# A linear-attention and feed-forward kernel on one core: the hand-written start in another order

## The chip, the cores and the metric

The kernel runs on one core of a Trainium2 chip. The metric is device time in microseconds, from three runs of the same program. A core has a matrix engine (TensorE, PE in the rows, with PEld for its weight loads), a vector engine (VectorE, DVE), an activation engine (ScalarE, ACT), a general engine (GpSimd, POOL), and a queue that issues transfers (SyncE, SP). Each engine runs its own instructions strictly in the order in which they were written; the engines meet only through semaphores.

## The reference, cut to what matters

```
# attention: 4 x 8 heads, 768 steps, head dimension 48, float32
for t in range(S):
    cur = einsum('bhd,bhe->bhde', u * k[t], v[t])
    y[t] = einsum('bhd,bhde->bhe', r[t], state + cur)
    state = w[t] * state + einsum('bhd,bhe->bhde', k[t], v[t])
# feed-forward on the 3072 rows of y, 384 wide
h = x @ w_in            # 384 x 2048
out = (h * cos(h)) @ w_out
```

## The kernel before

The 768 steps are cut into chunks of 128; 4 batches give 24 chunks, and two chunks make a block (256 rows of x, 12 blocks). Inside a chunk the recurrence becomes matrix products: a backward and a forward scan of the decays on VectorE (L283, L289), a multiplication of k and r by the decays (L298), scores on TensorE (L374), a mask (L335 on GpSimd, L393 on VectorE) and the product with v (L479, L485). The state that a chunk passes on is a product of transposed keys and v (L444). The block's result lands in two PSUM banks called py; ScalarE copies them to the tile xT as the upper half of x (L171), and the rest is made as the lower half (L528 with L531, or L174 on VectorE).

The feed-forward goes over 16 slices of the weights (weight 0 to 15; two of them make a unit of the first product). A slice is fetched packed (L180) and unpacked by ScalarE (L191, L195, L171) and VectorE (L203, L205), or for weight 1 by TensorE and ScalarE (L211, L212, L216). The first product is L594 (tile ph), the gate h*cos(h) runs over ScalarE (L557), VectorE (L560), ScalarE (L573), VectorE (L574), the second product is L612.

The first 135 us or so are ordered by hand: the string START is a list of tokens that are carried out one after the other, and each writes its instructions to the ends of their engines' queues. The words used below, with the number of a chunk, block or weight behind them:

- `ld` loads a chunk, `e` and `f` are the backward and forward scan, `q` the product r*k (L272), `k` and `r` the products with the decays, all on VectorE; `pc` the bonus sums on TensorE (L311), `cd` their copy on ScalarE, `c` the bonus sum on VectorE for later chunks (L325); `a` the scores, `A` the mask on GpSimd, `P` its use on VectorE;
- `t` transposes the keys on TensorE (L408), `K` copies them on ScalarE (tile kn), `s` makes the state's sums on TensorE (L444), `n` copies them on ScalarE (L452); `o` is the product with v; `xh`, `xp`, `xa`, `xl` make the two halves of x;
- `wl`, `wg`, `wy`, `wc`, `wx` are the steps of a weight in this order (ScalarE, ScalarE, VectorE, ScalarE, VectorE), `wp` and `wv` stand for `wx` where TensorE makes it; `raw` and `v` issue transfers on SP;
- `m0.3` and `m1.3` are the two halves of the first product of unit 3, `I S N M H L` the gate's steps, `mm2.3` the second product; `D6` is six products into a bank that nobody reads.

Unit 0 and 1 belong to block 0 (weights 0, 1 and 2, 3), unit 2 and 3 to block 1 with the same weights. So the first product can start when x of block 0 (chunks 0 and 1) is there, and its unit 2 when x of block 1 (chunks 2 and 3) is there. Four buffers hold v: that of chunk 3 is loaded into the one that `s0` reads first.

Of the kernel before, what the change touches and what calls it, by code (L numbers as in the profile page):

```python
# [993 lines left out]
```

## Time and profile before

| | |
|---|---|
| median of 3 runs | 497.75 us (497.69 to 498.51) |
| the profiled execution, its own time | 497.51 us |
| its span in the trace | 495.7 us |
| TensorE, VectorE, ScalarE, GpSimd busy | 98%, 79%, 52%, 44% of the span |
| granted TensorE clock | 1.00 in every slice of the page |

The span is the part that the trace covers; 1.8 us of the execution's own time lie outside it. Busy TensorE is not TensorE at its peak, since matmuls are pipelined and their ends are modelled: what counts is the time from one group's start to the next, and the waits. Names in the rows are without buffer numbers; a row with x14 merges fourteen instructions, and its second column is the time from the first one's start to the last one's end. Engines overlap neighbouring instructions by some 0.1 us, so the step from one start to the next is a little shorter than an instruction's time.

### The profile page before, as it was taken

What the parts mean: (1) busy time and instruction counts of PE and PEld (TensorE: products, weight loads), DVE (VectorE), ACT (ScalarE), POOL (GpSimd) and SP (SyncE); (2) the same over time, 40 slices, a digit from 0 to 9 for tenths busy, and PEclk for the clock granted to TensorE, in tenths of its full rate; (3) what the DMA queues carried; (4) which work ended last, traced back from release to release, by engine and by line L of the source; (5) the groups of instructions that cost most, each with busy time, mean ns of one, the idle gap of its engine ahead of it and who ended that gap; (6) DMA issues with size and microseconds to landing.
All of it is one profiled execution on the core that took longest, in us unless ns stands there. A gap on an engine that the chain in (4) does not pass through costs nothing.

```text
span 495.7 us, 13535 instructions
## 1 busy us (share of the span) xinstructions
PE 486.5 (98%) x5560; PEld 471.9 (95%) x5560; DVE 393.6 (79%) x681; ACT 257.9 (52%) x444; POOL 216.5 (44%) x280
## 2 busy tenths in 40 slices
PE   8999999999999999999999999999999999999996
PEld 7789999999999899999999999999999999999996
DVE  7999899988979779869868968967966957587632
ACT  3899988445344444354445345345435535534542
POOL 5138798344336335244435344433624523432330
PEclk9999999999999999999999999999999999999999
DMA  8998830234454153153162150342222212023001
GB/s 284 414 395 298 343 104 9 60 104 127 124 165 122 20 196 80 18 199 78 17 197 54 45 198 19 78 125 91 73 94 107 65 32 98 33 67 126 34 1 36
DMA packets 46289, 58.59 MB, mean 118 GB/s; under 512 B 30736, under 2 KB 37392, under 8 KB 46224
## 3 DMA queue, kind: packets, MB, share of 16 engines
q1 hardware_dynamic: 46080, 57.59, 35.5%
q8 instruction: 45, 0.74, 0.6%
q14 instruction: 20, 0.16, 0.1%
q10 hardware_dynamic: 144, 0.10, 0.1%
HBM read 49.80 MB, written 4.72 MB: 110 GB/s over the span
## 4 chain that ended last, share of the span: by engine, by line
PE 75%; DVE 13%; ACT 4%; SPq 2%; DMA 2%; issue 2%; POOL 0%; DVEq 0%; ACTq 0%
PE ph L594 34%; PE acc L612 32%; PE pa L382 2%; PE py L479 2%; DVE rr L560 2%; DVE rr L574 2%; SPq L425 2%; PE py L485 2%; DVE tt L289 1%; PE py L513 1%; DVE h L203 1%; PE pst L444 1%; DVE ee L283 1%; ACT rr L557 1%; DMA tt<-tr 1%
## 5 line engine op out<-in xcount | busy, mean ns | idle before, releaser
L174 POOL TENSOR_TENSOR gs<-rr,gs 128x256 fp32r<-128x256 f32 x188 | 160.8, 877 | 221.9 <-ACT gs L171 215.3
L594 PE MATMUL ph<-xT,w 128*128 128x256 f32 x1728 | 219.5, 281 | 1.2 <-DVE rr L574 0.6
L594 PEld LDWEIGHTS ph<-xT,w 128*128 128x128 f32 x1728 | 212.3, 188 | 5.3 <-PE py L513 1.9
L612 PE MATMUL acc<-w,gs 128*128 128x384 f32 x1152 | 214.9, 337 | 0.0
L612 PEld LDWEIGHTS acc<-w,gs 128*128 128x128 f32 x1152 | 196.3, 188 | 0.1
L573 ACT ACTIVATE rr<-rr,quarter 128x512 f32<-128x512 f32 x96 | 69.5, 724 | 91.3 <-DVE rr L560 91.2
L560 DVE SCALAR_TENSOR_TENSOR rr<-rr,ph 128x512 f32<-128x512 int32 x96 | 65.5, 683 | 49.8 <-ACT rr L557 49.2
L171 ACT CAST gs<-rr 128x512 fp32r<-128x512 f32 x92 | 57.1, 620 | 72.7 <-DVE rr L574 49.2
L574 DVE TENSOR_TENSOR rr<-rr,ph 128x512 f32<-128x512 f32 x96 | 65.0, 678 | 21.3 <-ACT rr L573 19.3
L557 ACT ACTIVATE rr<-ph 128x512 int32<-128x512 f32 x96 | 57.2, 596 | 41.6 <-PE ph L594 41.1
L335 POOL TENSOR_SCALAR_AFFINE_SELECT asb<-cd 128x512 f32<-128x512 f32 x48 | 34.6, 745 | 42.5 <-DVE cd L325 24.3
L396 DVE COPY_PREDICATED asb<-turned_mask,pa 64x128 f32<-64x128 uint8 (+1 forms) x108 | 33.6, 346 | 2.1 <-POOL asb L335 0.3
L283 DVE TENSOR_TENSOR_SCAN ee<-tt,one_e 112x516 f32<-112x516 f32 (+1 forms) x25 | 32.9, 1315 | 1.7 <-DMA tt<-tr 1.7
L289 DVE TENSOR_TENSOR_SCAN tt<-tt,inj 112x516 f32<-112x516 f32 x24 | 30.3, 1263 | 0.8
L174 DVE TENSOR_TENSOR xT<-py,xT 128x384 fp32r<-128x384 f32 x22 | 11.3, 551 | 14.0 <-ACT xT L171 14.0
L195 ACT ACTIVATE top<-raw 128x768 f16<-128x768 bf16 x16 | 17.3, 1088 | 3.6 <-DMA raw<-wts 2.9
L479 PE MATMUL py<-asb,v 128*32 128x128 f32 x384 | 18.0, 276 | 0.3 <-DVE asb L393 0.2
L485 PE MATMUL py<-asb,v 128*32 128x128 f32 x384 | 17.3, 273 | 0.0
L203 DVE CUSTOM_DVE_ANT_0 h<-h,top 128x1536 uint16<-128x1536 uint16 x16 | 16.4, 1022 | 0.6 <-ACT h L191 0.6
L171 ACT CAST xT<-py 128x384 fp32r<-128x384 f32 x24 | 10.5, 481 | 9.3 <-PE py L513 5.1
L171 ACT COPY past<-dd 48x192 f32<-48x192 f32 x40 | 14.0, 349 | 2.7 <-DVE dd L358 2.4
L382 PEld LDWEIGHTS pa<-tt 48*64 48x64 f32 x576 | 12.9, 134 | 2.2 <-issue 2.0
(94 smaller groups left out, 358.5 us busy)
## 6 DMA issues: line engine op xcount, KB each, us to landing
tt<-tr SPq DMA_DIRECT2D x22, 770.5 KB, 7.1
raw<-wts SPq DMA_DIRECT2D x16, 767.8 KB, 7.3
rk<-tn SPq DMA_DIRECT2D x20, 384.0 KB, 4.5
v<-tv SPq DMA_DIRECT2D x24, 224.0 KB, 4.4
ww<-w SPq DMA_DIRECT2D x6, 768.0 KB, 4.5
out<-ob SPq DMA_DIRECT2D x23, 192.0 KB, 2.1
top<-tt SPq DMA_DIRECT2D x112, 16.0 KB, 1.8
top<-tt SPq DMA_DIRECT2D x112, 8.0 KB, 1.8
```

Of the source, the lines that this page charges most:

```text
L171: (nc.scalar.copy if E[name] is nc.scalar else E[name].tensor_copy)(out=out, in_=in_)
L174: E[name].tensor_tensor(out=out, in0=full, in1=high.bitcast(F32), op=ALU.subtract)
L283: nc.vector.tensor_tensor_scan(out=ee[:, pairs].rearrange("p a t -> p (a t)")[:, ::-1], data0=wp[:, cols][:, ::-1], data1=one_e[:, pairs]. ...
L289: nc.vector.tensor_tensor_scan(out=wp[:, 0:W129], data0=wp[:, 0:W129], data1=inj.rearrange("p a t -> p (a t)"), initial=0.0, op0=ALU.mult, ...
L335: nc.gpsimd.affine_select(out=asb, in_=col.unsqueeze(2).to_broadcast([C, NP, C]), pattern=[[0, 4], [1, C]], compare_op=ALU.is_equal, fill= ...
L396: nc.vector.copy_predicated(*(which(x) for x in (a["asb", h], turned_mask, pa[h])))
L557: nc.scalar.activation(made["rr"].bitcast(I32), ph, AF.Copy, scale=INV2PI / W_SCALE, bias=0.25)
L560: nc.vector.scalar_tensor_tensor(out=made["rr"], in0=made["rr"].bitcast(I32), scalar=-2.0 * math.pi * W_SCALE, in1=ph, op0=ALU.mult, op1=A ...
L573: N=lambda: nc.scalar.activation(made["rr"], made["rr"], AF.Sin, scale=1.0 / W_SCALE, bias=quarter),
L574: M=lambda: nc.vector.tensor_tensor(out=made["rr"], in0=made["rr"], in1=ph, op=ALU.mult), H=high, L=low)
L594: nc.tensor.matmul(out=ph[:, fi], lhsT=wgt[u * FU + fi][:, 0, a, kt * 128:(kt + 1) * 128], rhs=xT[:, b, kt], start=n == 0, stop=n == 3 * K ...
L612: nc.tensor.matmul(out=accs[i][j][:, :DM], lhsT=gs[:, a, fi, j * C:(j + 1) * C], rhs=wgt[u * FU + fi][:, 1, b], start=u == 0 and fi == 0 a ...
```

## The change

Only START changes. Two lines of it show the first part:

```
-ld0 e0 f0 ld1 raw2 raw1 q0 e1 k0 D14 pc0 r0 q1 cd0 v0 v1 raw0 f1 D10 a0 W0 wg2 wl2 A0 k1 pc1 wl1 r1 wy2 P0 cd1 D6 a1
+ld0 e0 f0 ld1 raw2 raw1 q0 k0 r0 e1 D14 pc0 cd0 v0 v1 raw0 f1 q1 D10 a0 W0 wg2 A0 k1 pc1 cd1 wl2 r1 P0 wl1 wy2 D6 a1
```

On VectorE chunk 0's `k0 r0` come ahead of chunk 1's `e1`, `q1` goes behind `f1`, `P0` ahead of `wy2`, and `wy0` ahead of `e3 q3`. On TensorE `t0 t1 s0` go from ahead of unit 0 to behind it, `wp1` ahead of `xp0.0`, and twelve new idle products, `D12`, stand in the place of `t0 t1`. ScalarE takes `cd1` ahead of `wl2`, both `xh` of block 0 ahead of `wc0`, and `K0 K1` and `n0` go to either side of `I0`. GpSimd's order stays. SP's stays until the transfers of v for chunks 6 and 7, which go behind others (they are not needed before 150 us).

TensorE, from the second filler ahead of `a1` to block 0's lower half, before (pt is `t0 t1`, py `o0` and then `xp0.0`, pst `s0`):

```order
L740 MATMUL filled<-ident 128x128 x6
L374 MATMUL pa<-tt 128x128 x8
L408 MATMUL pt<-ident,tt 128x112 x8
L479 MATMUL py<-asb,v 32x128 x8
L485 MATMUL py<-asb,v 32x128 x8
L479 MATMUL py<-asb,v 32x128 x4
L485 MATMUL py<-asb,v 32x128 x4
L479 MATMUL py<-asb,v 32x128 x4
L485 MATMUL py<-asb,v 32x128 x4
L528 MATMUL py<-xT,nident 128x384
L444 MATMUL pst<-v,kn 32x48 x2
```

The same engine and place after (left is `wp1`, ph with w_302 and w_262 are the halves of unit 0):

```order
L740 MATMUL filled<-ident 128x128 x12
L479 MATMUL py<-asb,v 32x128 x8
L485 MATMUL py<-asb,v 32x128 x8
L479 MATMUL py<-asb,v 32x128 x4
L485 MATMUL py<-asb,v 32x128 x4
L479 MATMUL py<-asb,v 32x128 x4
L485 MATMUL py<-asb,v 32x128 x4
L211 MATMUL left<-h,ident 128x384
L212 MATMUL left<-w_262,nident 128x384
L211 MATMUL left<-h,ident 128x384
L212 MATMUL left<-w_262,nident 128x384
L528 MATMUL py<-xT,nident 128x384 x2
```

The transposes and the state's sums have left this stretch, and follow unit 0; a row of L740 counts a product once that the trace counts as two instructions.

ScalarE, around the first `I0` (L557), before (L531 is `xa0.1`, L452 `n0`, L195 and L191 `wg3 wl3`, cd `cd2 cd3`, kn `K3 K2`):

```order
L531 CAST xT<-py 128x384
L452 COPY all_states<-pst 48x192 x4
L557 ACTIVATE rr<-ph 128x512
L195 ACTIVATE top_100<-raw 128x768
L191 ACTIVATE h<-raw 128x768
L171 COPY cd<-pc 128x8 x2
```

and after (the first kn is `K0 K1`, which stood far ahead before):

```order
L531 CAST xT<-py 128x384 x2
L216 CAST w_262<-left 128x384 x2
L171 COPY kn<-pt 128x384 x2
L557 ACTIVATE rr<-ph 128x512
L452 COPY all_states<-pst 48x192 x4
L195 ACTIVATE top_100<-raw 128x768
L191 ACTIVATE h<-raw 128x768
L171 COPY cd<-pc 128x8 x2
```

`K0 K1` and `n0` now stand between block 0's lower half and `wg3`, and `n0` behind `I0`.

The second part lies at unit 10. On VectorE (L560 is `S10`, L574 `M10`, L203 `wy13`, L325 `c4`, L393 `P5`):

```order
-L560 SCALAR_TENSOR_TENSOR rr<-rr,ph 128x512
-L203 ISA h<-h,top_100 128x1536
-L574 TENSOR_TENSOR rr<-rr,ph 128x512
+L205 TENSOR_TENSOR w_1076<-h,w_1076 128x2x384
+L560 SCALAR_TENSOR_TENSOR rr<-rr,ph 128x512
+L325 TENSOR_REDUCE cd<-rk 128x8
+L574 TENSOR_TENSOR rr<-rr,ph 128x512
+L203 ISA h<-h,top_100 128x1536
 L393 COPY_PREDICATED asb<-mask,pa 128x512 x2
 L560 SCALAR_TENSOR_TENSOR rr<-rr,ph 128x512
```

The bonus sum of chunk 4 takes the place between the two gate steps that weight 13's first step had; before, it came six instructions later, behind `r4`. On ScalarE `wg15` changes places with `wc13`. The transfers that turn chunk 4's keys (`t4`, L425) write the buffer that `c4` reads, and wait for it.

## Rows read from the trace of the kernel before

**Rows 1.** Table by stage: start:end, length, busy us of PE, PEld, DVE, ACT, POOL; clock, DMA share, GB/s.
```profile
10.00:36.00 26.00, 24.13 (x418) 20.65 (x417) 25.43 (x37) 22.31 (x43) 5.79 (x7) 1.00 1.01 404
```
**Rows 2.** TensorE's waits, a row: waiting line, what ended it, us in total, times, longest.
```profile
PE ph L594 <- DVE rr L574: 0.6, 1, 0.6
```
**Rows 3.** VectorE in order of time, 7 to 12 us: start, us, instruction.
```profile
7.28 1.23 DVE L283 TENSOR_TENSOR_SCAN ee<-tt,one_e 112x516 f32<-112x516 f32 x1 [0.64 <-DMA tt<-tr]
8.43 1.05 DVE L298 TENSOR_TENSOR tt<-tt,ee 112x512 f32<-112x512 f32 x1
9.41 1.11 DVE L298 TENSOR_TENSOR tt<-tt 112x512 f32<-112x512 f32 x1
10.45 0.68 DVE L272 TENSOR_TENSOR rkt<-tt 112x512 f32<-112x512 f32 x1
```
**Rows 4.** GpSimd in order of time: the masks of chunk 0.
```profile
8.02 1.96 POOL L335 TENSOR_SCALAR_AFFINE_SELECT asb<-cd 128x512 f32<-128x512 f32 x2 [2.02 <-ACT cd L171]
```
**Rows 5.** TensorE in order of time, 11 to 27 us.
```profile
11.67 1.05 PE L311 MATMUL pc<-u_by_head,rkt 112*128 112x2 f32 x8
12.58 1.58 PE L740 MATMUL filled<-ident 128*128 128x128 f32 x12
...
15.24 1.22 PE L408 MATMUL pt<-ident,tt 112*128 112x112 f32 x8
16.39 0.64 PE L479 MATMUL py<-asb,v 128*32 128x128 f32 x16
...
19.08 0.87 PE L444 MATMUL pst<-v,kn 128*32 128x48 f32 x64
19.88 0.91 PE L211 MATMUL left<-h,ident 128*128 128x384 f32 x2
...
21.63 0.95 PE L311 MATMUL pc<-u_by_head,rkt 112*128 112x2 f32 x8
...
23.79 1.93 PE L594 MATMUL ph<-xT,w 128*128 128x256 f32 x14 [0.23 <-ACT xT L531]
...
26.37 0.58 PE L408 MATMUL pt<-ident,tt 112*128 112x112 f32 x4
```
**Rows 6.** ScalarE in order of time, 17 to 36 us.
```profile
17.18 0.83 ACT L171 COPY kn<-pt 128x384 f32<-128x384 f32 x2
18.18 0.48 ACT L171 CAST xT<-py 128x384 fp32r<-128x384 f32 x1 [0.17 <-PE py L479]
...
23.61 1.29 ACT L452 COPY all_states<-pst 48x192 f32<-48x192 f32 x4
25.75 0.60 ACT L557 ACTIVATE rr<-ph 128x512 int32<-128x512 f32 x1 [0.85 <-PE ph L594]
26.25 1.09 ACT L195 ACTIVATE top<-raw 128x768 f16<-128x768 bf16 x1
...
34.28 0.86 ACT L171 CAST xT<-py 128x384 fp32r<-128x384 f32 x2
```
**Rows 7.** TensorE in order of time at the start of unit 2.
```profile
36.03 1.21 PE L594 MATMUL ph<-xT,w 128*128 128x256 f32 x8 [0.44 <-ACT wholes L171]
```
**Rows 8.** SP in order of time: v of chunks 2 and 3; the time includes a wait.
```profile
13.21 6.80 SPq L266 DMA_DIRECT2D v<-tv  x2
```
**Rows 9.** The page: DMA issues, KB each, median us from issue to landing.
```profile
raw<-wts SPq DMA_DIRECT2D x16, 767.8 KB, 7.3
```
**Rows 10.** VectorE in order of time, around unit 10's gate: `wy13`, then `M10`.
```profile
75.62 1.47 DVE L203 CUSTOM_DVE_ANT_0 h<-h,top 128x1536 uint16<-128x1536 uint16 x1
77.01 0.68 DVE L574 TENSOR_TENSOR rr<-rr,ph 128x512 f32<-128x512 f32 x1
```
**Rows 11.** In order of time: a gate step, `N10` on ScalarE; `c4`'s old place on VectorE.
```profile
63.47 0.60 ACT L557 ACTIVATE rr<-ph 128x512 int32<-128x512 f32 x1 [0.63 <-PE ph L594]
...
75.74 0.73 ACT L573 ACTIVATE rr<-rr,quarter 128x512 f32<-128x512 f32 x1 [0.75 <-DVE rr L560]
...
83.91 0.54 DVE L325 TENSOR_REDUCE cd<-rk 128x8 f32<-128x384 f32 x1
```

More of the change, by code (lines that the diff above doesn't have):

```diff
@@ L66 @@
 START = """
-ld0 e0 f0 ld1 raw2 raw1 q0 e1 k0 D14 pc0 r0 q1 cd0 v0 v1 raw0 f1 D10 a0 W0 wg2 wl2 A0 k1 pc1 wl1 r1 wy2 P0 cd1 D6 a1
-wc2 t0 wg1 A1 ld3 ld2 wg0 W1 t1 P1 v5 wx2 wy1 o0 K0 K1 xh0.0 xp0.0 s0 wl0 e3 q3 wc1 xa0.0 wy0 wc0 xh0.1 wp1 f3 pc3
-xp0.1 wv1 wx0 xa0.1 q2 e2 n0 k3 f2 raw3 k2 m0.0 m1.0 pc2 t3 r3 I0 r2 wg3 raw4 v2 wl3 cd2 v3 raw5 wy3 m0.1 cd3 S0 t2 a3
-A3 K3 K2 A2 P3 ld7 wl4 wg4 a2 ld5 wc3 wg5 N0 raw8 raw6 P2 s1 wx3 raw9 n1 o1 xh1.0 xl1.0 raw7 lr5 v4 ld4 m1.1 xh1.1
+ld0 e0 f0 ld1 raw2 raw1 q0 k0 r0 e1 D14 pc0 cd0 v0 v1 raw0 f1 q1 D10 a0 W0 wg2 A0 k1 pc1 cd1 wl2 r1 P0 wl1 wy2 D6 a1
+A1 wg1 wc2 D12 ld3 ld2 wg0 W1 P1 v5 wx2 wl0 wy1 wc1 o0 xh0.0 xh0.1 wy0 wc0 e3 wp1 xp0.0 xp0.1 wx0 xa0.0 xa0.1 wv1 q3
+f3 m0.0 m1.0 t0 t1 K0 K1 pc3 s0 q2 e2 k3 f2 raw3 k2 pc2 t3 r3 I0 n0 r2 wg3 raw4 v2 wl3 cd2 v3 raw5 wy3 m0.1 cd3 S0 t2
+a3 A3 K3 K2 A2 P3 ld7 wl4 wg4 a2 ld5 wc3 wg5 N0 raw8 raw6 P2 s1 wx3 raw9 n1 o1 xh1.0 xl1.0 raw7 lr5 v4 ld4 m1.1 xh1.1
 xl1.1 M0 m0.2 wl5 Wa3 I1 wy4 m1.2 S1 m0.3 H0 wc4 N1 wy5 wc5 wg6 I2 m1.3 M1 wx4 wl6 I3 Hv1 L0 mm2.0 m0.4 wx5 S2 N2 wy6
@@ L75 @@
 M8 I9 wc11 wy10 wg12 wc10 mm2.6 mm2.7 raw15 t5 d4 S9 N9 H8 m4 u4 r5 wx11 a5 wx10 M9 wl12 wl13 H9 L8 L9 m0.10 wy12 wc12
-m1.10 wg13 m0.11 I10 k4 wx12 S10 wy13 m1.11 N10 mm2.8 I11 M10 P5 wc13 wg15 wl15 Wa5 W4 d5 S11 wx13 N11 M11 f4 m0.12 r4
-c4 H10 L10 wg14 mm2.9 m1.12 m0.13 H11 t4 wl14 I12 S12 N12 pp4 pp5 wy15 m1.13 a4 L11 A4 M12 P4 I13 wy14 wcv15 S13 wx15
+m1.10 wg13 m0.11 I10 k4 wx12 S10 c4 m1.11 N10 mm2.8 I11 M10 wy13 P5 wg15 wc13 wl15 Wa5 W4 d5 S11 wx13 N11 M11 f4 m0.12
+r4 H10 L10 wg14 mm2.9 m1.12 m0.13 H11 t4 wl14 I12 S12 N12 pp4 pp5 wy15 m1.13 a4 L11 A4 M12 P4 I13 wy14 wcv15 S13 wx15
 mm2.10 wc14 mm2.11 o2 p2 N13 wx14 K5 m0.14 H12 m1.14 M13 m0.15 L12 xh2.0 Hv13 e6 k6 t6 m1.15 I14 S14 K4 N14 M14 mm2.12
```

## The prediction

> **What bounds the kernel now.** I read the table by stage first. Between 10 and 36 us VectorE is busy for 25.43 of 26 us, TensorE for 24.13, ScalarE for 22.31, and the DMA queues are full at 404 GB/s [rows 1]: in the start several engines are at their limit together, so a step gained on one can be lost on the next. The list of TensorE's waits then shows how little is left to take later: 0.6 us for a gate step of VectorE, once [rows 2], and 0.4 us at unit 2 put down to ScalarE's small copy called wholes [rows 7]. Behind block 0's first product TensorE runs one instruction behind the other, and over the whole span it is busy for 98%. So the end moves by what TensorE's long row of work is pushed or pulled, and the question is at which moment the row becomes unbroken, and which waits stand in it behind that. The views by time, engine by engine, show the moments: the row starts for good at 23.79 us, when the last quarter of block 0's x has come from ScalarE, and unit 0 ends 1.93 later, at 25.72 [rows 5].
>
> **VectorE's and TensorE's start.** Before, the scan `e1` waits 0.64 us for its transfer, ending at 7.28, and chunk 0's products `k0 r0` follow while GpSimd makes chunk 0's masks (8.02 to 9.98): they take 1.05 and 1.11 us. `q1`, a product of the same size that begins after the masks, takes 0.68 [rows 3, 4]. After, `k0 r0` go into that wait and lie before the masks: from 6.64 two steps of 0.6 (0.68 less the overlap of neighbours) end at 7.84. Then `e1` (step 1.15, from 7.28 to 8.43), 0.2 for the small reciprocal that a forward scan has ahead of it, `f1` as long as `e1`, and `q1`: 7.84 + 1.15 + 0.2 + 1.15 = 10.34, end 11.02. Before, `q1` ended at 11.13 without `f1`. So VectorE has gained a scan, 1.2 us, but the product that TensorE waits for next has gained only 0.1. `pc1` began at 11.67, since the scores `a0` stood ahead of it and waited for `r0` (end 10.52); `r0` is early now, and `pc1` can begin at 11.1, 0.55 earlier.
>
> From there TensorE's steps of before hold: from `pc1` to the place of `t0` 3.57 us (11.67 to 15.24), which gives 14.65. There `D12` stands now: the twelve instructions of `D6` took 1.58 [rows 5], so twenty-four take at most twice that, 3.16, and less by the end of the pipeline, which counts once and not twice, an estimated 0.3: I take 2.8. `o0` begins at 17.45 instead of 16.39. It is 1.06 later although its inputs are early; of the idle products every instruction counts, and nothing hides them. From `o0`'s start to `xh0.0` it was 1.79 (16.39 to 18.18) [rows 5, 6], so `xh0.0` begins at 19.25, while TensorE does `wp1` (19.88 to 21.63, 1.75) [rows 5]: 19.25 to 21.0. The two products of the lower half follow, some 0.4 each, and ScalarE's copies `xa0.0 xa0.1`, about 0.5 each as `xh0.0` [rows 6], partly beside them: ready at 22.1. Plus 1.93: unit 0 ends at 24.05, 1.65 us earlier than at 25.72. That gain is real, but it is made by putting work behind unit 0.
>
> **What comes behind unit 0.** On TensorE `t0 t1` (four transposes take 0.58, some 0.4 of it ahead of the next instruction), `pc3` (0.9, as `pc1`) and `s0` (0.80, from 19.08 to 19.88) [rows 5]: 2.4 us or a little more, so `s0` ends at 26.45, where before unit 0 had just ended, at 25.72: TensorE is later by 0.7 or 0.8. On ScalarE `K0 K1` (0.83), then `I0`, then `n0` (1.29), which must wait for `s0` [rows 6]. Before, `n0` filled the wait of ScalarE for unit 0 (23.61 to 24.90, with 0.85 of idle behind it): it cost nothing. Now it begins at 26.45 and `wg3`, the weight step behind it, at about 27.65 instead of 26.25: +1.4. Behind `wg3` ScalarE has had no rest up to `xh1.0` at 34.28, the copy of block 1's x, for which unit 2 waits; the little idle time in between gives back 0.2 at most, and `xh1.0` comes at 35.4 to 35.6. The masks of chunks 2 and 3 wait for `cd2 cd3`, copies in the same row of ScalarE, but end before `xh1.0`.
>
> The transfer of v for chunk 3 goes into the buffer that `s0` reads. Before, SP waited in the pair of v transfers, from 13.21 to 20.01 [rows 8]; now the wait lasts until `s0` has begun to read, about 25.9. Everything behind it in SP's row is issued up to 5.9 us later; the weight for `wg5`, which needs it at about 32.7, is the first at risk. By the median row, 7.3 us from issue to landing [rows 9], it would land at 33.6 and hold ScalarE 0.9; but that is the row of a full queue. This queue has run empty by then, and 767.8 KB at 404 GB/s are 1.9 us [rows 1, 9], so I take 30 to 31 and cost it at nothing; the end of the range is 0.9.
>
> **Unit 2.** Before, its row goes on at 36.03, ended by "ACT wholes" [rows 7], but that small copy feeds no product; x was ready at 35.14 (`xh1`, 34.28 + 0.86 [rows 6]). What holds the engine for these 0.9 us I can't read. Two bounds: if it is something that runs beside, and doesn't come later with x, the products wait only for x, 1.2 later than before, and TensorE loses 0.6 to 0.7 (its fifth product, on the lower half of x, goes from 36.4 to 37.05). If it follows x, the loss is the whole 1.2. The first is nearer to the 0.7 or 0.8 that TensorE already has from the moved work, so that both limits meet there.
>
> **Chunk 4's bonus sum.** `M10` on VectorE needs `N10`, which ends at 75.74 + 0.73 = 76.47 [rows 11]; before, it waited for `wy13` (75.62, 1.47 us), and ran from 77.01 [rows 10]. With `c4` (0.54 [rows 11]) in that place VectorE is free before `N10` ends, and `M10` begins at 76.52: 0.49 earlier. TensorE waits for it, 0.6 us [rows 2], so all of 0.49 is TensorE's. Could the start's loss vanish in this same wait, because TensorE comes to it later and VectorE doesn't? No: ahead of it the gate's first step on ScalarE waits 0.63 for TensorE's product (63.47 [rows 11]), so the gate goes with TensorE, and both are late alike. The bounds are 0, if VectorE comes 0.5 later than TensorE, and 0.5. `wy13` moves back by 1.1 and catches up when `c4`'s old place is reached at 83.91. `wg15` and `wc13` change places on ScalarE; `wc13` waits for `wy13`, so this is at zero.
>
> **The sum.** +0.7 (start) − 0.5 (gate) = +0.2 with the gap at unit 2 hidden, +1.2 − 0.5 = +0.7 with it not. The profiled execution took 497.51 us, 0.24 less than the median, 497.75. Against 497.51 the two are 497.7 and 498.2; the middle is 498.0, which I forecast. It is 0.25 above the median. A measurement of this kernel can tell about 0.2%, 1.0 us, from no change; this is inside. Its own range is 497.3 to 498.7.
>
> **Rivals.**
>
> *Faster: unit 0's gain survives.* If ScalarE were not late behind `n0`, because `K0 K1` and `s0` come sooner than I have it (x ready 1.65 earlier), x of block 1 would not be later, and VectorE's gained scan could bring it sooner by up to half of its 1.2 us (the other half goes where VectorE waits for TensorE's scores): the start would give −0.5, and with the gate −1.0 against 497.51: 496.5 to 496.7. For it: 1.65 us at unit 0, the largest single figure here. Against it: `n0` needs `s0`, and its 1.29 have lost their cover.
>
> *Slower: the scan under the masks.* The trace shows VectorE slowed beside the masks: 1.05 and 1.11 against 0.68 [rows 3, 4]. After, `e1` and `f1` run there. A scan with half a microsecond of overlap kept its 1.23 (`e1`, 7.28 to 8.51), hence my sum. But if `f1` is held until the masks end at 9.98 instead of starting at 9.19, then `q1`, `pc1`, unit 0, `s0`, `n0` and `xh1` are 0.8 later, all in one row: 498.0 + 0.8 = 498.8, up to 499.2 with the gap at unit 2 whole. It decides when the scans lose 0.75 together. The Trainium skill has a rule for this, in "SBUF — State Buffer", section "Who interferes with whom": a VectorE instruction with two inputs in SBUF contends with a GpSimd instruction that reads SBUF, and the shared port is an exclusive lock. By an exclusive lock `k0` would have been held at 8.43 until the first or second mask was over; it took 0.4 longer, not 1.5, so the row is nearer to a shared slowdown. By the rule the sum would be 498.8, by the row 498.0.
>
> *Slower: the queue.* SP held by v of chunk 3 until 25.9, and the weight for `wg5` late by 0.9: 498.9. It decides from a landing after 32.7 on. For it: the median row; against it: the empty queue.
>
> *Neither part does anything.* The moved steps find the same waits in another order: the median again, 497.75, inside my own range too.
>
> **Chances.** My sum and no effect at all, together 0.56; unit 0's gain survives 0.20; the scan under the masks 0.14; the queue 0.10. So faster 0.20, same 0.56, slower 0.24, and the range takes in nearly all of both sides: 496.6 to 499.2.
>
> **What would show it.** In the changed kernel's rows: `k0 r0` at 0.68 and ahead of `e1`, `f1` at 1.23 and `q1` ending by 11.1; twenty-four idle instructions from 14.65 to 17.45; unit 0's end at 24.05; `n0` at 26.45 and `wg3` at 27.65, with no wait between it and `xh1.0` at 35.4 to 35.6; v of chunk 3 issued at 25.9; in TensorE's waits, the one for L574 down from 0.6 to 0.2 or less. The forecast is wrong if `wg3` begins before 27, if `q1` ends after 11.8, or if unit 2 goes on before 36.2 or after 37.3.

## The result, and the profile after

The changed kernel takes 502.70 us (median of 6 runs, 502.19 to 504.54), against 497.76 before (497.49 to 498.51). The ratio is 1.0101, with a 95% interval from 1.0088 to 1.0114: 4.9 us slower, outside the range of 496.6 to 499.2. The profiled execution of the changed kernel took 503.11 us, with a span of 501.4 (before 497.51, with 495.7), so the traces lie 5.6 us apart, 0.7 more than the medians.

How late TensorE is, step by step, is read by comparing the start of the same product of the feed-forward (L594) in both traces:

| at product of L594 | before | after | later by |
|---|---|---|---|
| first of unit 0 | 22.93 | 22.20 | −0.73 |
| first of unit 1 | 26.72 | 28.62 | 1.89 |
| first of unit 2 | 35.32 | 39.03 | 3.71 |
| first of unit 3 | 38.13 | 41.33 | 3.20 |
| first of unit 8 | 61.17 | 65.14 | 3.97 |
| first of unit 12, behind unit 10's gate | 77.84 | 81.36 | 3.52 |
| first of units 13 and 14 | 82.11, 92.70 | 86.75, 97.81 | 4.63, 5.11 |
| from there to 360 us | | | 4.65 to 5.16 |
| last unit | 480.77 | 486.48 | 5.71 |

So nearly everything happens in the first 93 us: 1.9 before unit 1, 1.3 from there to unit 3, 0.8 more between units 6 and 7, where VectorE is full, and 1.1 net around unit 10, where the change was meant to gain. The last 0.6 come in one step, at 368 us of the trace before.

TensorE's rows by time, in the order start, duration, instruction, with the idle time ahead of it in brackets (they answer to [rows 5, 7]):

```profile
22.20 2.84 PE L594 MATMUL ph<-xT,w 128*128 128x256 f32 x18
...
30.96 2.06 PE L374 MATMUL pa<-tt 48*128 48x128 f32 x32 [0.67 <-ACT cd L171]
...
34.96 0.38 PE L479 MATMUL py<-asb,v 128*32 128x128 f32 x2
37.30 0.31 PE L479 MATMUL py<-asb,v 128*32 128x128 f32 x3 [1.96 <-issue]
...
37.87 5.72 PE L594 MATMUL ph<-xT,w 128*128 128x256 f32 x45
```

Unit 0 ends at 25.04 (22.20 + 2.84), earlier than before as forecast, though by 0.7 and not by 1.65. The third and fourth rows are the surprise. In the middle of chunk 2's product with v TensorE stands for 2 us, and "issue" says that it waited for nothing that the profile shows. Behind it nothing is left to wait for: 45 products run in one piece.

ScalarE and VectorE in the same stretch (ScalarE's rows answer to [rows 6], the third one is block 1's x):

```profile
27.50 1.29 ACT L452 COPY all_states<-pst 48x192 f32<-48x192 f32 x4 [0.67 <-PE pst L444]
28.81 1.10 ACT L195 ACTIVATE top<-raw 128x768 f16<-128x768 bf16 x1
...
38.00 0.87 ACT L171 CAST xT<-py 128x384 fp32r<-128x384 f32 x2 [1.13 <-PE py L485]
```
```profile
34.77 0.93 DVE L205 TENSOR_TENSOR w<-h,w 128x768 fp32r<-128x768 f32 x1
38.51 1.02 DVE L174 TENSOR_TENSOR xT<-py,xT 128x384 fp32r<-128x384 f32 x2 [2.81 <-ACT xT L171]
```

`n0` has a wait of 0.67 ahead of it and `wg3` comes at 28.81, as the forecast's step had it but 1.1 later. `xh1.0` comes at 38.00 and not at 35.5: ScalarE waits for the product that TensorE halted in. VectorE, which before was busy for 39.19 of the 41 us from 36 to 77, stands idle for 2.81 us. Before, the same row had 0.47:

```profile
34.79 1.02 DVE L174 TENSOR_TENSOR xT<-py,xT 128x384 fp32r<-128x384 f32 x2 [0.47 <-ACT xT L171]
```

VectorE and GpSimd at the front (they answer to [rows 3, 4]):

```profile
6.85 0.69 DVE L298 TENSOR_TENSOR tt<-tt,ee 112x512 f32<-112x512 f32 x1
7.46 0.68 DVE L298 TENSOR_TENSOR tt<-tt 112x512 f32<-112x512 f32 x1
8.06 1.22 DVE L283 TENSOR_TENSOR_SCAN ee<-tt,one_e 112x516 f32<-112x516 f32 x1
9.32 0.18 DVE L288 RECIPROCAL inj<-ee 112x4 f32<-112x4 f32 x1
9.54 1.26 DVE L289 TENSOR_TENSOR_SCAN tt<-tt,inj 112x516 f32<-112x516 f32 x1
10.72 1.05 DVE L272 TENSOR_TENSOR rkt<-tt 112x512 f32<-112x512 f32 x1
```
```profile
8.42 2.81 POOL L335 TENSOR_SCALAR_AFFINE_SELECT asb<-cd 128x512 f32<-128x512 f32 x2 [2.59 <-ACT cd L171]
```

`k0 r0` take 0.69 and 0.68 and the scans keep their time; what pays are the masks, 2.81 instead of 1.96, and `q1`, 1.05 instead of 0.68.

Around unit 10, ScalarE's `wg15` and `N11` and TensorE's wait behind it (these answer to [rows 10, 11]):

```profile
82.59 1.09 ACT L195 ACTIVATE top<-raw 128x768 f16<-128x768 bf16 x1 [1.62 <-issue]
83.54 0.81 ACT L171 CAST w<-h 128x768 fp32r<-128x768 f32 x1
84.26 0.91 ACT L191 ACTIVATE h<-raw 128x768 int32<-128x768 uint32 x1
85.07 0.18 ACT L171 COPY wholes<-ee 112x4 f32<-112x4 f32 x1
85.16 0.72 ACT L573 ACTIVATE rr<-rr,quarter 128x512 f32<-128x512 f32 x1
```
```profile
81.13 1.38 DVE L203 CUSTOM_DVE_ANT_0 h<-h,top 128x1536 uint16<-128x1536 uint16 x1
```
```profile
86.74 2.34 PE L594 MATMUL ph<-xT,w 128*128 128x256 f32 x18 [0.72 <-DVE inj L288]
```

`wg15` writes the tile `top` from which `wy13` reads, and begins 0.08 us after `wy13` has ended (82.51). Everything queued behind it, `N11` too, is late.

### The profile page after: what moved, and what is told of

Same layout as the page of the kernel before. It is cut to its first block, busy times and chain, and to the rows that moved or that the text cites. A ratio compares the mean times of both kernels' runs of the same rounds, so it can differ in the third digit from the quotient of the medians.

```text
span 501.4 us, 13583 instructions
## 1 busy us (share of the span) xinstructions
PE 489.8 (98%) x5584; PEld 475.3 (95%) x5584; DVE 391.6 (78%) x681; ACT 258.4 (52%) x444; POOL 217.6 (43%) x280
## 4 chain that ended last, share of the span: by engine, by line
PE 67%; DVE 9%; ACT 3%; issue 2%; SPq 0%; POOL 0%; DMA 0%; DVEq 0%; ACTq 0%
PE acc L612 30%; PE ph L594 29%; PE pa L382 2%; DVE rr L560 2%; PE py L479 2%; DVE rr L574 2%; PE py L485 1%; PE py L513 1%; DVE tt L289 1%; DVE asb L396 1%; PE pst L444 1%; ACT rr L557 1%; ACT rr L573 1%; PE py L507 1%; DVE tt L300 1%
## 5 line engine op out<-in xcount | busy, mean ns | idle before, releaser
L594 PE MATMUL ph<-xT,w 128*128 128x256 f32 x1728 | 220.3, 281 | 1.2 <-DVE inj L288 0.7
L594 PEld LDWEIGHTS ph<-xT,w 128*128 128x128 f32 x1728 | 212.5, 188 | 5.6 <-PE py L513 1.6
L560 DVE SCALAR_TENSOR_TENSOR rr<-rr,ph 128x512 f32<-128x512 int32 x96 | 65.5, 683 | 49.3 <-ACT rr L557 48.5
L171 ACT CAST gs<-rr 128x512 fp32r<-128x512 f32 x92 | 57.1, 620 | 71.2 <-DVE rr L574 49.7
L574 DVE TENSOR_TENSOR rr<-rr,ph 128x512 f32<-128x512 f32 x96 | 64.9, 677 | 22.3 <-ACT rr L573 20.4
L557 ACT ACTIVATE rr<-ph 128x512 int32<-128x512 f32 x96 | 57.2, 596 | 42.5 <-PE ph L594 41.9
L195 ACT ACTIVATE top<-raw 128x768 f16<-128x768 bf16 x16 | 17.5, 1092 | 4.7 <-DMA raw<-wts 2.4
L171 ACT CAST xT<-py 128x384 fp32r<-128x384 f32 x24 | 10.5, 481 | 13.6 <-PE py L513 8.3
L203 DVE CUSTOM_DVE_ANT_0 h<-h,top 128x1536 uint16<-128x1536 uint16 x16 | 16.1, 1007 | 1.4 <-ACT h L191 1.2
L205 DVE TENSOR_TENSOR w<-h,w 128x768 fp32r<-128x768 f32 x15 | 14.8, 1000 | 0.9 <-ACT w L171 0.8
L171 ACT COPY past<-dd 48x192 f32<-48x192 f32 x40 | 14.0, 349 | 2.7 <-DVE dd L358 2.4
```

The costliest lines, as they stand in the source:

```text
L171: (nc.scalar.copy if E[name] is nc.scalar else E[name].tensor_copy)(out=out, in_=in_)
L557: nc.scalar.activation(made["rr"].bitcast(I32), ph, AF.Copy, scale=INV2PI / W_SCALE, bias=0.25)
L560: nc.vector.scalar_tensor_tensor(out=made["rr"], in0=made["rr"].bitcast(I32), scalar=-2.0 * math.pi * W_SCALE, in1=ph, op0=ALU.mult, op1=A ...
L574: M=lambda: nc.vector.tensor_tensor(out=made["rr"], in0=made["rr"], in1=ph, op=ALU.mult), H=high, L=low)
L594: nc.tensor.matmul(out=ph[:, fi], lhsT=wgt[u * FU + fi][:, 0, a, kt * 128:(kt + 1) * 128], rhs=xT[:, b, kt], start=n == 0, stop=n == 3 * K ...
```

## TensorE's instructions come in blocks

The trace also holds transfers of another kind than data: 45 packets of 16 KB in a queue marked "instruction", for the some 11,250 instructions of TensorE that the trace counts, one for every 250. The halt lies behind the 960th of them in both kernels. From the trace, for the kernels that tell it best (all but the first two are described below, under these names): when the 704th (one block earlier) was issued, when the packet that came next began and ended, when the 960th was issued, when TensorE went on, and by how much that step is longer than the steady one:

| kernel | 704th | packet | 960th | goes on | halt |
|---|---|---|---|---|---|
| before | 30.79 | 33.57 to 34.64 | 35.32 | 36.04 | 0.60 |
| after | 31.96 | 34.97 to 35.92 | 35.08 | 37.31 | 2.22 |
| first_part | 31.58 | 34.55 to 35.49 | 34.69 | 36.94 | 2.24 |
| q1_early | 31.69 | 34.40 to 35.34 | 34.80 | 36.77 | 1.96 |
| after_queue | 31.82 | 34.59 to 35.53 | 34.93 | 37.00 | 2.06 |
| queue_free | 31.97 | 32.18 to 33.32 | 34.95 | | none |
| second_part | 30.33 | 34.00 to 34.94 | 34.85 | 36.42 | 1.45 |
| gate_first | 31.74 | 34.46 to 35.39 | 36.28 | 36.77 | 0.37 |
| vector_only | 31.14 | 33.71 to 34.65 | 35.67 | 36.11 | 0.32 |
| before_queue | 31.19 | 31.22 to 32.30 | 35.71 | | none |
| q3_fill | 31.61 | 33.88 to 34.95 | 35.24 | 36.30 | 1.05 |
| states_back | 37.98 | 40.43 to 41.36 | 40.79 | 42.61 | 1.71 |
| before_short | 31.88 | 34.41 to 35.37 | 37.87 | | none |
| before_early | 33.09 | 35.63 to 36.57 | 39.09 | | none |
| states_front | 32.33 | 33.69 to 34.77 | 36.85 | | none |

Wherever there is a halt, it ends 1.2 to 1.5 us after the packet. Wherever the packet ended more than 1.5 us ahead of the 960th instruction, there is none. In these rows the packet begins up to 3.7 us after the block before it was entered, when the queues are full of data (in before_trim, at an earlier block, 5.3); where they were not, it was 0.0 to 0.2 (before_queue, queue_free) and 0.5 to 0.7 (53 us and 70 us in the kernel before). The wait also differs between executions: before, second_part and gate_first have the same order up to 75 us and halt for 0.60, 1.45 and 0.37 us.

The place isn't special to chunk 2 or unit 2. Of the changed kernel's waits of TensorE, one more is put down to "issue":

```profile
PE py L513 <- issue: 0.6, 1, 0.6
```

It lies at 372 us, behind the 8896th instruction, which is 31 times 256 behind the 960th, and ends 1.4 us after a packet. It is the step of 0.6 in the table above, and about the 0.7 by which the traces differ more than the medians. Halts at L513 in other kernels lie just so: behind the 3008th and the 7872nd instruction in before_early, the 4032nd in second_part and states_warm, the 5056th in first_part. Between the 704th and the 960th instruction TensorE needs 4.5 us in the kernel before and 3.1 in the changed one, since `D12` puts 48 instructions (24 products, 24 weight loads) ahead and with that the block's end out of the slow products of unit 2 into the short ones of chunk 2.

The Trainium skill has this in "Runtime: NRT & Kernel Launch", section "Instruction fetch mechanics": blocks of 16 KB, 256 instructions, fetched while the engine runs. It says that the cost of crossing a block is "mostly hidden". The size agrees with the packets here; the cost doesn't: the crossing at 35 us takes 0.3 to 2.2 us in ten of the fifteen kernels of the table.

## The experiments

Each diff shows tokens of START, from the first to the last that moved; a ratio is against the kernel before on the same chip, with its 95% interval. The names in brackets are those that the table above and the text use. One execution of each kernel was traced.

**The two parts** (first_part, second_part).

```diff
-S10 c4 m1.11 N10 mm2.8 I11 M10 wy13 P5 wg15 wc13 wl15
+S10 wy13 m1.11 N10 mm2.8 I11 M10 P5 wc13 wg15 wl15
```

(in the changed kernel, and `c4` behind `r4` again)

> The changed kernel with its second part undone: weight 13's first step, chunk 4's bonus sum and weight 15's first step stand around unit 10 as before the change. Theory: in the changed kernel ScalarE's first step of weight 15 (L195, 82.59 us) stood 1.62 us behind weight 13's first step on VectorE, and unit 11's gate step behind it came late, so that TensorE lost 1.1 us at 86.7 and won only 0.45 at 81.4. Without the second part the time falls by 0.5 to 1.2 us, to 501.5 to 502.2. Rival, the prediction's term: the second part is worth 0.5 us, and without it the time rises to 503.2.

Measured 501.98 us, 1.0080 (1.0054 to 1.0105): 0.7 less than with the second part (1.0101, 1.0088 to 1.0114). The two intervals overlap a little.

The other way round, the same lines with - and + exchanged, in the kernel before:

> The kernel before with the second part of the change alone. Theory: the wait of TensorE for L574 of unit 10 falls from 0.6 to about 0.2 us, and a new wait of 0.7 to 1 us for unit 11's gate stands some 5 us behind it: 498.2 to 498.9, 0.5 to 1.1 slower than before. Rival, the prediction's term: 497.3, faster by 0.5.

Measured 498.77 us against 497.88, 1.0014 (1.0000 to 1.0029). At unit 10 TensorE gains 0.57 in its trace, and behind it loses 1.11 and 0.48. Each of the two differences is near the limit of what can be told, but they agree on 0.7 to 0.9 us of loss, and both traces have it in the same waits. So the prediction's term has the wrong sign.

**The idle products** (no_idle).

```diff
-A1 wg1 wc2 D12 ld3 ld2
+A1 wg1 wc2 ld3 ld2
```

> The changed kernel without the twelve idle products D12. Theory: TensorE's halt of 2.2 us at 35.1 in the changed kernel and its halt of 0.6 us at 35.3 before are one and the same: it falls behind the same number of its instructions (the 480th product or so of the program) in both, 1.4 us after a 16 KB transfer of instructions landed. Without D12 the place lies 24 products further on in the program, among the slower products of unit 2, and the halt is 0.4 to 1.0 us there; with that the time falls by 1.2 to 2.8 us, to 500 to 501.5. Rival A: the halt belongs to the work at that place (the products of scores and v of chunk 2, or SP's burst of transfers); it stays at 2 us in the same products, and the time falls by 1 us at most. Rival B: the idle products lie on the path with their whole 2.8 us and nothing else; the time falls by 2.8 with the halt of 2.2 unchanged.

Measured 500.34 us, 1.0045 (1.0032 to 1.0058): 2.4 faster than the changed kernel. The halt is gone from chunk 2's product, where rivals A and B had it. The 960th instruction lies in unit 2 now (37.02); there TensorE has a step that is 0.7 too long, which is the wait for x, and a second one of 0.4 right behind the 960th, which the profile puts down to x too. But the copy of x (36.11, two of them in 0.86) had ended at 36.97, and this step ends at 37.44, 1.3 us after the packet (35.21 to 36.14), as the halts do: some 0.3 us of halt are left, a little less than expected. Compared with the changed kernel, TensorE is 0.80 us earlier at unit 1 (27.81) and 1.89 earlier at unit 3 (39.44): 0.8 is the start that `D12` made late, and 1.1 comes in the stretch with the halt.

**VectorE's front** (q1_early, vector_only).

```diff
-e1 D14 pc0 cd0 v0 v1 raw0 f1 q1 D10
+e1 q1 D14 pc0 cd0 v0 v1 raw0 f1 D10
```

> The changed kernel with chunk 1's product q1 on VectorE directly behind the backward scan e1, ahead of the forward scan f1 (before the change it stood there too). Theory: q1 was 0.75 us later than forecast because the masks on GpSimd and the work with two inputs on VectorE slow each other (masks 2.81 us instead of 1.96, q1 1.05 instead of 0.68); ahead of f1 it ends near 10.1 instead of 11.77, chunk 1's bonus sums on TensorE begin at 11.35 right behind the scores instead of at 11.83, and unit 0 ends 0.4 to 0.5 earlier than at 25.04. The time falls by 0.2 to 0.6 us if that reaches the end, and stays if the halts behind it are fixed by transfers. Rival: q1's place costs nothing, because chunk 1's scores wait for the forward scan anyway, which now ends 0.7 later: no change at unit 0.

Measured 502.46 us, 1.0093 (1.0058 to 1.0128), 0.24 less than the changed kernel and not told from it. In the trace `pc1` begins at 11.56 and unit 0 ends at 24.77, 0.27 earlier: a little over half of what was expected.

```diff
-q0 e1 k0 D14 pc0 r0 q1 cd0 v0 v1 raw0 f1 D10
+q0 k0 r0 e1 D14 pc0 cd0 v0 v1 raw0 f1 q1 D10
```

(in the kernel before)

> The kernel before with VectorE's part of the change in chunks 0 and 1 alone: k0 r0 ahead of e1, q1 behind f1. Theory: q1 ends 0.6 us later than before, because the scans and the masks on GpSimd slow each other, r1 0.5 us earlier; chunk 1's bonus sums on TensorE begin 0.1 to 0.2 later, its scores at the same time; no more than 0.3 us either way, 497.5 to 498.1. Rival, the slower case of the prediction: VectorE loses 0.8 us under the masks and the end with it, 498.5. Other rival: VectorE's gained 1.2 us reach block 1's x, 497.2 or less.

Measured 497.68 us, 0.9993 (0.9980 to 1.0007): no difference. In its trace `f1` takes 1.64, `q1` 1.05 and the masks 2.15, as masks and scans meet there too, and it costs nothing at the end.

**The queue** (queue_free, before_queue, after_queue).

```diff
-raw5 wy3 m0.1 cd3 S0 t2 a3 A3 K3 K2 A2 P3 ld7
+raw5 raw9 wy3 m0.1 cd3 S0 t2 a3 A3 K3 K2 A2 P3 ld7
```

(`raw9` leaves its old place)

> The changed kernel with one transfer of SP in another place: the packed weight 9 stands directly behind weight 5, where it holds SP until its buffer is free (33.5 us in the changed kernel), so that the loads of chunks 5 and 7 and the weights 6 and 8 are issued only then and the queues are nearly empty from 32 us on. TensorE's instructions are the same in number and order. Theory: the halt of 2 us in chunk 2's product with v is TensorE waiting for its next 16 KB of instructions, whose transfer stands 3 us in queues full of data; with the queues empty it lands by 34 us instead of 35.9, and the halt falls to 0.5 us or less. Block 1's x is then bound by ScalarE, 1 us earlier than at 38.0; the time falls by 0.5 to 1.2 us unless the weights 6 and 8 come late. Rival: the halt belongs to the products at that place, or to their number per microsecond; it stays at 2 us.

TensorE's order is that of the changed kernel, word for word, and the halt is gone:

```profile
34.96 0.44 PE L479 MATMUL py<-asb,v 128*32 128x128 f32 x8
35.18 0.44 PE L485 MATMUL py<-asb,v 128*32 128x128 f32 x8
35.55 1.33 PE L594 MATMUL ph<-xT,w 128*128 128x256 f32 x9
37.70 4.47 PE L594 MATMUL ph<-xT,w 128*128 128x256 f32 x31 [0.82 <-ACT xT L171]
```

The time is 506.55 us, 1.0181 (1.0163 to 1.0200), because a weight that was held back is missed, as ScalarE's row shows:

```profile
46.63 1.09 ACT L195 ACTIVATE top<-raw 128x768 f16<-128x768 bf16 x1 [4.07 <-DMA raw<-wts]
```

The mechanism is shown by this; its worth at the end is not. Up to that wait its worth can be read: the two traces agree to 0.01 us up to unit 1 (28.61 in both), block 1's x then comes at 37.16 instead of 38.00, and unit 3 begins at 40.49 instead of 41.33. So up to there the halt of 2.2 us costs 0.84; without it ScalarE's own row holds x, and VectorE still stands idle for 1.97. Then one transfer less was moved, in both kernels:

```diff
-raw8 raw6 P2 s1 wx3 raw9
+raw9 raw6 P2 s1 wx3 raw8
```

> The kernel before with the transfers of the packed weights 8 and 9 exchanged in SP's row: weight 9, which waits for ScalarE's step of weight 5 (30.8 us), holds back weight 6 and weight 8, which were issued at 28.1. TensorE's instructions are untouched. Theory: with one load in flight instead of three when TensorE asks for its next block of instructions at 30.8, the block lands by 33.5 instead of 34.64, and the halt of 0.6 us at unit 2 is 0 to 0.2; weight 6 arrives as before, weight 8 3 us later, which nobody notices. 497.0 to 497.4, faster by 0.3 to 0.7. Rival: the block waits behind the transfers that are issued at 30.8 all the same; the halt stays and so does the time.

> The changed kernel with the same exchange of weights 8 and 9 in SP's row; here weight 9 is free at 33.5 us, and TensorE asks for its block at 32.0 with two loads of chunks in flight. Theory: the block's transfer begins before 34 instead of at 34.97, the halt of 2.2 us in chunk 2's product with v falls to 0.5 to 1.5, and the time falls by 0.5 to 1.2 us, to 501.5 to 502.2, unless weight 6, 2 us later, is missed on ScalarE. Rival: no change in the halt.

In the kernel before the packet begins at once (31.22) and the halt is gone, but the time is 498.26 us, 1.0012 (0.9999 to 1.0025): no gain. TensorE is 0.5 earlier at unit 2 than it would have been, and has given it back by unit 7 (0.12 earlier than in the kernel before at unit 3, 0.40 later at unit 7), where the gate's engines set the pace. In the changed kernel the packet still waits until 34.59, with the two loads of chunks in flight, the halt stays at 2.06, and so does the time, 502.64 us, 1.0097 (1.0082 to 1.0112). Here the rival was right.

**Fewer idle products in the kernel before** (before_short, before_early, before_trim).

```diff
-cd1 D6 a1
+cd1 a1
```

> The kernel before without the six idle products D6 ahead of chunk 1's scores. Theory: the halt of 0.6 us at 35.3 (shown against ACT wholes) is the same wait for instructions. Twelve products and twelve weight loads fewer ahead of it put the place 12 products of unit 2 later in the program, 1.4 us later in time, and the halt there falls to 0 to 0.2 us; the scores a1 begin 0.4 us earlier at most, since they wait for VectorE. 496.9 to 497.4, faster by 0.3 to 0.8. Rival: the halt belongs to unit 2's start (the small copy, or x's second half) and stays at 0.6 in the same product: no change.

```diff
-q0 e1 k0 D14 pc0
+q0 e1 k0 D8 pc0
```

> The kernel before with eight instead of fourteen idle products ahead of pc0 (24 instructions of TensorE fewer, in a place where nothing waits for their end but chunk 0's bonus sums). Theory: the place where TensorE runs out of instructions lies 12 products further on in unit 2, and the halt of 0.6 us at 35.3 falls to 0 to 0.2, with the clock at 1.00 unlike in the kernel without D6; 496.9 to 497.5. Rival: the first idle products are needed for the clock, and the granted clock is 0.5 in part of the first 20 us: 498.5 or more.

In both the halt at unit 2 is gone, as expected. But the times spread: 496.9 to 500.7 and 496.5 to 500.6, with medians of 499.16 (1.0031, 1.0007 to 1.0056) and 498.42 (1.0010, 0.9989 to 1.0031). The table by stage of the first, from its run of 498.32 us, shows one cause (the column ahead of the last two is the granted clock):

```profile
12.00:14.00 2.00, 1.00 (x13) 0.91 (x14) 2.00 (x4) 1.98 (x3) 0.00 (x0) 1.00 1.07 431
14.00:16.00 2.00, 1.63 (x19) 1.44 (x16) 2.00 (x4) 1.85 (x4) 1.36 (x3) 0.75 1.01 422
16.00:18.00 2.00, 2.00 (x29) 1.64 (x31) 2.00 (x4) 1.88 (x4) 0.00 (x0) 0.50 1.03 419
```

TensorE had stood for half of the stretch from 12 to 14 us, and the clock was granted at 0.50, the lower of its two levels (1.2 of 2.4 GHz), in most of the next 4 us. How much of the spread this is isn't shown: over the whole run the mean granted clock was 0.994 in the longest run, of 500.70 us, but 1.00 in one of 499.14. In the second the twenty idle instructions behind `pc0` run at half the pace, 4.62 us instead of 2.48 in the kernel before, although the clock column reads 1.00 there:

```profile
8.23 4.62 PE L740 MATMUL filled<-ident 128*128 128x128 f32 x20
```

Why they do stays open.

A third version took one product from each of the three groups (D13, D9, D5 for D14, D10, D6):

> The kernel before with one idle product fewer in each of its three groups (D13, D9, D5: 12 instructions of TensorE fewer ahead of unit 2, with no pause longer than 0.25 us more). Theory: the place where TensorE runs out of instructions lies 6 products further on in unit 2, 0.7 us later in time, and the halt of 0.6 us at 35.3 falls to 0 to 0.2; with the clock kept in every run the time is 497.0 to 497.4. Rival: even so much less idle work lets the clock fall in some runs, and the median is 498 or more; or the halt moves with the product and there is no change.

Measured 498.56 us, 1.0021 (0.9999 to 1.0043), from 497.4 to 502.6. In the traced run, of 498.97 us, the clock is at 1.00 throughout, and the halt of this kind has moved one block ahead, into `s0`:

```profile
18.71 0.70 PE L444 MATMUL pst<-v,kn 128*32 128x48 f32 x46
21.45 0.41 PE L444 MATMUL pst<-v,kn 128*16 128x48 f32 x18 [2.04 <-issue]
```

The packet ran from 19.02 to 20.06 there; it is the 448th instruction. The block before it was entered at 13.72, 0.4 us earlier than in the kernel before (14.10), but the packet began only 5.3 us behind that, where it was 1.3 before. The theory looked at the block of unit 2 alone. The rival's first half is borne out: the three longest of the eleven runs, 500.46 to 502.55 us, have a mean granted clock of 0.992 to 0.993, the other eight 0.994 to 1.00.

**The states** (states_front, states_warm, q3_fill, states_back). In the changed kernel without second part and `D12`, the transposes, the states' sums and their copies go in front again (`n0` leaves its place behind `I0`):

```diff
-D6 a1 A1 wg1
+D6 a1 t0 t1 A1 wg1
-o0 xh0.0 xh0.1 wy0 wc0 e3 wp1 xp0.0 xp0.1 wx0 xa0.0 xa0.1 wv1 q3 f3 m0.0 m1.0 t0 t1 K0 K1 pc3 s0 q2
+o0 K0 K1 xh0.0 xh0.1 wy0 wc0 e3 wp1 s0 xp0.0 xp0.1 wx0 xa0.0 xa0.1 wv1 n0 q3 f3 m0.0 m1.0 pc3 q2
```

> The changed kernel without its second part and without D12, and with the transposes t0 t1, the state's sums s0 and their copies K0 K1 n0 in front of unit 0 again (s0 behind wp1, n0 behind the copies of block 0's lower half); all else as after the change. Theory: what is left of the loss without D12 and without the second part (1.8 us, 499.6) is that n0 lies on ScalarE between unit 0 and wg3, with a wait of 0.67 us for s0 ahead of it, and everything behind is late up to block 1's x. With n0 in ScalarE's wait for unit 0 again the time is 497.2 to 498.2. Rival: VectorE's new order or the place of wp1 and xh is what is left: 499.2 or more.

Measured 499.36 us, 1.0039 (1.0018 to 1.0060). The rival's number; but the granted clock was 0.67 and 0.50 from 26 to 30 us. With idle products in TensorE's two pauses (`D3` ahead of `wp1`, `D2` ahead of `t3`):

> As the kernel with the states in front again (changed kernel without second part and D12, states in front of unit 0), with three idle products ahead of wp1 and two ahead of t3, in the two places where TensorE stood there for 0.78 and 0.48 us. In that kernel's profile the granted clock was 0.67 and 0.50 between 26 and 30 us, behind the second of them. Theory: that kernel's 499.36 was the clock and not the order; with the clock at 1.00 throughout the time is 497.2 to 498.3. Rival: the order of VectorE, wp1 and xh costs 1.5 us by itself: the clock is 1.00 and the time 499 or more.

The clock is 1.00 and the time 499.18 us, 1.0024 (1.0011 to 1.0037). So the rival holds, and without the second part, without `D12` and with the states in front, 1.5 us of loss remain. In VectorE's rows of this kernel:

```profile
22.16 0.96 DVE L205 TENSOR_TENSOR w<-h,w 128x768 fp32r<-128x768 f32 x1 [0.93 <-ACT w L171]
...
28.67 1.05 DVE L298 TENSOR_TENSOR tt<-tt,ee 112x512 f32<-112x512 f32 x1
```

Weight 0's last step waits for `wc0`, which ScalarE now makes behind both `xh`, and `k2` (the second row) ends at 29.72; TensorE's `t2`, which needs it, begins at 29.82. Before, `t2` began at 27.89. With `q3` directly behind `e3`, in VectorE's pause:

> The kernel with the states in front again and five more idle products (changed kernel without second part and D12), with chunk 3's product q3 on VectorE directly behind the scan e3, where VectorE stood there for 0.93 us waiting for ScalarE's copy for weight 0. Theory: what is left of the loss in that kernel, 1.5 us, is VectorE: weight 0's last step (L205, 22.16) waits for a copy that ScalarE now makes behind K0 K1 and both xh, the product k2 ends at 29.7 instead of 27.8, and chunk 2's transposes wait for it. With q3 in the idle time k2 and the transposes come 0.5 us sooner, and the time falls by 0.3 to 0.6 us, to 498.6 to 498.9. Rival: the transposes wait for something else; no change, 499.2.

`t2` begins at 28.48, of which 0.8 us is a start that was earlier as a whole, and 0.55 the edit. The time is 499.01 us, 1.0020 (1.0010 to 1.0030), not told from 499.18; the halt in this profile is 1.05 long, where there was none in the one before. The wait is shown, its share of the 1.5 us is not.

The move of the states alone, in the kernel before (`K0 K1`, `s0` and `n0` leave their old places):

```diff
-D6 a1 wc2 t0 wg1 A1 ld3 ld2 wg0 W1 t1 P1
+D6 a1 wc2 D4 wg1 A1 ld3 ld2 wg0 W1 P1
-m0.0 m1.0 pc2 t3 r3 I0 r2 wg3
+m0.0 m1.0 t0 t1 K0 K1 s0 pc2 t3 r3 I0 n0 r2 wg3
```

> One part of the change alone: the kernel before with t0 t1, s0 on TensorE behind unit 0, K0 K1 on ScalarE ahead of I0 and n0 behind I0, and four idle products in the place of t0 t1. VectorE's order, wp1 and the xh copies stay as before. Theory: on ScalarE n0 loses its cover, with a wait for s0 ahead of it, wg3 and all behind it up to block 1's x are late by 1.5 to 2.5 us, and so is TensorE: 499.2 to 500.3. Rival: the loss of the first part is only the halt for instructions and VectorE's start, and this move alone costs 0.5 at most: 497.8 to 498.3.

Measured 504.80 us, 1.0142 (1.0105 to 1.0178), far more than either theory. A row of ScalarE and one of TensorE tell the order of events:

```profile
27.50 0.86 ACT L171 COPY kn<-pt 128x384 f32<-128x384 f32 x2 [3.50 <-PE pt L408]
```
```profile
32.44 0.60 PE L408 MATMUL pt<-ident,tt 112*128 112x112 f32 x4 [2.51 <-ACT cd L171]
```

ScalarE stands 3.5 us for `t0 t1`; then `n0`, `wg3`, `wl3` lie ahead of `cd2`, and `t3` waits 2.5 us for `cd2`. Behind each of TensorE's pauses the clock is at 0.50 in a stretch (24 to 26 and 34 to 36 us). In the changed kernel the same wait stands at chunk 3's scores, 0.67 us.

**The gate** (gate_first, gate_trim). In the kernel before with the second part, `N11` one place ahead:

```diff
-wg15 wc13 wl15 Wa5 W4 d5 S11 wx13 N11 M11
+wg15 wc13 Wa5 W4 d5 S11 wx13 N11 wl15 M11
```

> The kernel before with the second part of the change, and on ScalarE unit 11's gate step N11 (L573) one place further ahead, before weight 15's second step wl15 (L191). Theory: the second part loses because ScalarE stands at wg15 until VectorE has read the tile top of weight 13, and N11 is queued behind wg15, wc13, wl15. With N11 ahead of wl15 it begins 0.8 us sooner, TensorE's new wait of 0.7 us behind VectorE's L288 (0.9 against the steady row) falls to 0 to 0.3, the next wait at L374 to 0, and the gain at unit 10 stays: 497.0 to 497.6. Rival: VectorE itself is late by weight 13's step in its new place; the wait stays at 0.7, 498.4 to 499.

Measured 498.16 us, 1.0002 (0.9990 to 1.0014). TensorE's new wait falls from 0.88 to 0.23 against the steady row and the one at L374 from 0.50 to 0.16, as expected; the time is 0.6 below that of second_part, whose interval overlaps, and no faster than without the second part. A further version (with one product less in each idle group) takes `S11` directly behind `wy13`, `N11` directly behind `wg15`, `M11` ahead of `wx13`:

> As the kernel with one idle product fewer in each of the three groups, and with the second part of the change in another order: VectorE takes unit 11's first gate step S11 directly behind weight 13's first step and M11 ahead of weight 13's last, ScalarE takes N11 directly behind wg15. Theory: the wait at unit 10 falls as in the change (0.72 to 0.25 against the steady row), and the new wait at unit 11 doesn't arise, because nothing that waits for weight 13 stands ahead of N11 but wg15: 0.4 to 0.5 faster than the kernel with the idle products alone, 496.5 to 497.0. Rival: the masked copy P5, now behind S11, or weight 13's last step makes the next group late, and the gain goes there: no difference between the two.

Measured 498.40 us, 1.0017 (0.9996 to 1.0038), against 498.56 with the idle products alone: no difference. TensorE gains 0.47 at unit 10 and loses 0.85 at 80 us, 0.46 of it in one wait that its profile puts down to ScalarE's copy of a weight (L171). That is the rival.

No version was found that beats the kernel before.

## Why the prediction was wrong, step by step

The forecast had +0.7 us for the start and −0.5 for the gate. The start came out at 3.2 by unit 3, and the gate at +0.7 to +0.9. The sign that I had set for unit 2, a start after 37.3, came true: 39.03. Block 1's x, for which unit 2 waits, came at 38.00 and not at 35.5. Of these 2.5 us, 1.05 stand already at `n0`, which the front made late, and 1.13 are ScalarE's wait for the product in which TensorE halted; the rest is ScalarE's row between them.

**VectorE's front: the size of `q1`.** `q1` ended at 11.77 and not at 11.02. The front was 0.2 late by its loads, the steps around the scans took a little more, and `q1` itself 1.05 instead of 0.68. The scans weren't held, so the slower rival failed as it stood, although the lateness that it gave, 0.8, is nearly the measured 0.75. What I had read off [rows 3, 4], a slowdown that both share, fits only in part: the masks lost 0.85 us to the scans. That is nearer to the lock of which the Trainium skill speaks ("SBUF — State Buffer", "Who interferes with whom") than I allowed, with GpSimd as the one who waits here; in vector_only `f1` lost 0.4 as well. No run separates lock and shared slowdown: a later pair of the same masks took 1.22 (at 13.15 us), so the 1.96 was no undisturbed time either. At the end the front's price isn't told from nothing, by vector_only in the kernel before and by q1_early in the changed one.

**Unit 0: right in kind.** `D12` took 2.87 (forecast 2.8), unit 0 ended at 25.04 instead of 24.05; 0.7 of the 1.0 is there at `pc1` (11.83 instead of 11.1), from the front.

**Behind unit 0: right in kind, one wait left out.** `n0` began at 27.50 and `wg3` at 28.81 (forecast 26.45 and 27.65), late by the same 1.0 to 1.2. I had `cd2` late, but asked only when the masks would end; chunk 3's scores on TensorE wait for it too, 0.67 us. states_back shows how large that wait can be.

**The transfers: right.** v of chunk 3 was issued at 27.15 (forecast 25.9), weight 5 landed at 32.09 (forecast 30 to 31), and `wg5` began at 34.01 without a wait.

**Unit 2: the step that failed.** I wrote that I couldn't read what holds TensorE at 36.03, and bounded it by "runs beside" and "follows x", 0.6 to 1.2 us. It was the wait for a block of instructions, tied to a count of instructions and to the state of the queues. So the 48 instructions of `D12` were costed by their 2.8 us alone. They moved the block's end from behind block 1's x, where VectorE covers it (before_queue: taking it away gains nothing), to ahead of x, where VectorE stands idle with it. With no_idle, `D12` is 2.4 us of the 4.9. Up to unit 3 the traces split it: 0.8 for the later `o0`, which the forecast had, and 1.1 in the stretch with the halt, which it hadn't; queue_free, without the halt alone, gives 0.84 for the same.

**The gate: the gain right, the price left out.** M10 was worth 0.45 (forecast 0.49). But I put `wg15` and `wc13` at zero with the argument that `wc13` waits for `wy13` anyway, and didn't ask what `wg15` waits for, nor what stands behind it. It was −0.5 in the sum and came out at +0.7 to +0.9. Weight 13 has little slack: wherever its steps were put, TensorE lost what it had gained.

**What stays open.** 4.9 is 2.4 for `D12`, 0.7 for the second part, and 1.8 for the rest by subtraction, if the parts add up, which no run shows. Of the rest 1.5 stay with the states in front. The late `k2` behind ScalarE's reordered copies is a shown wait in that rest; its share wasn't separated.

## What to carry to other kernels

Before adding or moving many short matrix instructions, count where the blocks of instructions end, and look in the trace at the instruction packets: where an engine stands with "issue" or with a releaser that feeds it nothing, and the halt ends at a fixed time after such a packet (1.2 to 1.6 us here), the cost of an edit is the shift of that halt besides the edit's own time. In these runs an idle product was never only its time: it held the clock, it counted in the block, and too many or too few of them cost more than they filled. When a step is moved behind another because one engine is free there, list for each engine that reads or overwrites its tiles what stands behind that wait.
